# A planner's picture of its transfers: shared queues in place of fixed times

## The chip, the cores and the metric

The kernel runs on one core of a Trainium2 chip. The metric is the device time of one execution in microseconds (us), lower is better; a time is given as the median over runs.

## The reference

Attention in which a query only sees keys of the same hash bucket, followed by a feed-forward block with a gate (float32; 4 batches, 8 heads, sequence 768, head size 64; 3072 tokens, model width 512, inner width 2048):

```python
q_bits, k_bits = (q @ proj > 0), (k @ proj > 0)          # 6 bits each
mask = bucket(q_bits)[..., :, None] == bucket(k_bits)[..., None, :]
scores = where(mask, q @ k.T / sqrt(64), -1e9)
x = (softmax(scores) @ v)                                # to (3072, 512)
h = x @ w_in                                             # (3072, 2048)
g = h * erf(softplus(h))
out = g @ w_out                                          # (3072, 512)
```

## The kernel before, in words

**Two stages.** The attention (`attention`, 16 pairs of heads) is followed by the feed-forward (`feed_forward`), which works through six tiles `t` of 512 tokens. Both are written as lists of operations, each with an engine, a cost, the operations that it needs and a function that emits its instructions. A planner plays the list, and the operations are emitted in the order in which they came up. As every engine works through its instructions in order, this emission order is the order of each engine; the real waits between engines come from the data. So a planner's costs and times are nowhere waited for: they only decide what stands ahead of what on PE, DVE, ACT, POOL and SP. The attention is ordered by `arrange`, the feed-forward by `by_need`.

**`by_need` (lines 198 to 304).** For a margin it works out backward from the order of TensorE's products when each operation is due (`dates`), then plays the list forward (`play`): whenever an engine is free, it takes of the operations that are open the one due first (TensorE: the one of the lowest rank). It does so for three margins with five rounds each and keeps the order whose last TensorE operation ends soonest in the play. An operation opens when the operations in its `after` have ended, plus `late` of each of these where it is on another engine or `far` is set. A transfer is an operation on SP or POOL (its cost is the time to issue it) whose `late` is the time until its data has landed.

**The first product** `x @ w_in` is done in Strassen's manner (Winograd's form): seven products P1 to P7 of half size, the chain P1, P6, P2, P7, P4, P5, P3. For tile 0 these are plain (line 1444). For tiles 1 to 5 each of the seven is split again into seven small products (`small`, line 1683: 8 TensorE matmul instructions each in the trace). Their weights are 7 blocks for each step of the chain, 35 steps in all. These blocks are formed once, kept in DRAM, and read back for each step:

- `presum_inner` (line 1545, DVE) forms four of the seven blocks in a staging buffer. There are three: two in free rooms of `h`, one in `wt`, and the seven steps use them as 0, 1, 2, 0, 1, 2, 2. So P2, P5 and P3 go through `wt`, and P5's sums must wait until P2's have left.
- `keep` (line 1548, POOL) sends these four blocks (1.05 MB) to `wi_dram`; `keep_outer` (lines 1552 and 1553, SP, two issues) the other three for P6, P7, P5 and P3. `behind` puts the `keep` of P2, P4, P5 and P3 behind the first `load_wi` in the list.
- `load_wi` (line 1652, SP) reads the seven blocks of a step (1.835 MB) into a ring of two places in `w_in_sb`. A place is free when the products of two steps earlier are done; for the first two, when the plain products are done.
- `presum_xi` (line 1665, POOL) forms the sums of `x` for a step. `add_small` (lines 1710 on ACT and 1713 on DVE) takes each small product out of PSUM into `h`; PSUM has few banks for them, so a product waits for the addition of an earlier one.
- `add_far` (line 1720, POOL) adds a block of P5's result into `h` by an accumulating transfer, twice in a tile, with 512 KB each.

**The gate** (`gate_ops`: `lead` at line 1832 and `factor` at line 1840 on ACT, `multiply` at line 1847 on DVE) works on quarters of `h`. **The second product** `g @ w_out` (`project`, line 1987; 4 matmul instructions for each operation) of tile t runs interleaved with the first product of tile t + 1; in the later tiles three of its seven products are split again (`project_small`, line 2143), whose weight sums are kept by `keep_b` (line 2077, POOL) and read by `load_b` (line 2081, SP). `combine` (lines 2028 and 2030) adds the results and sends them out on SP (line 2036). `load_x` (line 447, SP) reads the `x` of the next tile.

Before, each of these transfers has a fixed `late`: `load_wi` 8.5 us (12.0 the first), `keep` 5.0, `keep_outer` 4.5, `add_far` 7.0, `keep_b` 5.0, `load_b` 7.0, `load_x` 6.0, whatever else is in flight.

Of the kernel before, what the change touches and what calls it, by code (L numbers as in the profile page):

```python
# [93 lines left out]
class Op:  # L94
# [13 lines left out]
    far: bool = False  # L108
    near: tuple = ()
    port: bool = False  # L110


TABLE_LOAD = 1.28
# [3 lines left out]
ROUNDS = 5  # L117
SHARED = 0.54
LENIENCE = 0.3


def arrange(ops, rooms, patience=0.0):
# [75 lines left out]
def by_need(ops, rooms, begin=None):  # L198

    names = {op.name: op for op in ops}
    users, needs = {}, {}
    for op in ops:
        needs[op.name] = {a for a in op.after if a in names}
        for a in needs[op.name]:
            users.setdefault(a, []).append(op)

    def away(a, op):
        return 0.0 if a.engine == op.engine and not a.far else a.late  # L210

    def dates(products, margin):
        starts, t = {}, 0.0
        for op in products:
            starts[op.name] = t
            t += op.cost
        left = {name: len(n) for name, n in needs.items()}
        sorted_ops, free = [], [op for op in ops if not left[op.name]]
        while free:
            op = free.pop()  # L220
            sorted_ops.append(op)
            for user in users.get(op.name, ()):
                left[user.name] -= 1
                if not left[user.name]:
                    free.append(user)
        due = {}
        for op in reversed(sorted_ops):
            due[op.name] = min(
                [starts.get(op.name, float("inf"))]
                + [due[user.name] - away(op, user) - user.cost - margin for user in users.get(op.name, ())]  # L230
            )
        return due

    def play(due):
        missing = {name: len(n) for name, n in needs.items()}
        opened = {}
        at, released, running = {}, {}, {}
        rings = {ring: [] for ring in rooms}
        table, now, order, ended = "exp", 0.0, [], 0.0
        for op in ops:  # L240
            opened.setdefault(op.engine, [])
            if not missing[op.name]:
                opened[op.engine].append(op)
                at[op.name] = 0.0

        def start_of(op):
            ring = rings[op.take[0]] if op.take else ()
            room = rooms[op.take[0]] if op.take else 1
            return max(at[op.name], released.get(ring[-room], float("inf")) if len(ring) >= room else 0.0)

        def place(op):
            return (op.rank if op.engine == "PE" else (due[op.name], op.rank)), op.name

        while len(order) < len(ops) or running:
            after = float("inf")
            for engine, entries in opened.items():
                if engine in running or not entries:
                    continue
                starts = [(start_of(op), op) for op in entries]
                first = max(min(start for start, _ in starts), now, (begin or {}).get(engine, 0.0))  # L260
                if first == float("inf"):
                    continue
                if first > now + 1e-9:
                    after = min(after, first)
                    continue
                op = min((op for start, op in starts if start <= first), key=place)
                cost = op.cost
                if op.table and op.table != table:
                    table = op.table
                    cost += TABLE_LOAD  # L270
                entries.remove(op)
                running[engine] = [op, cost]
                order.append(op)
                if op.take:
                    rings[op.take[0]].append(op.take)
            both = all(engine in running and running[engine][0].port for engine in ("DVE", "POOL"))
            pace = {engine: SHARED if both and running[engine][0].port else 1.0 for engine in running}
            after = min([after] + [now + rest / pace[engine] for engine, (_, rest) in running.items()])
            assert after < float("inf")
            for engine in list(running):  # L280
                running[engine][1] -= (after - now) * pace[engine]
                if running[engine][1] > 1e-9:
                    continue
                op = running.pop(engine)[0]
                if engine == "PE":
                    ended = after
                for what in op.free:
                    released[what] = after + op.late
                for user in users.get(op.name, ()):
                    at[user.name] = max(at.get(user.name, 0.0), after + away(op, user))  # L290
                    missing[user.name] -= 1
                    if not missing[user.name]:
                        opened[user.engine].append(user)
            now = after
        return order, ended

    best = None
    for margin in MARGINS:
        order = sorted(ops, key=lambda op: op.rank)
        for _ in range(ROUNDS):  # L300
            order, ended = play(dates([op for op in order if op.engine == "PE"], margin))
            if best is None or ended < best[0] - 0.05:
                best = ended, order
    return best[1]
@with_exitstack
def kernel(
# [34 lines left out]
    small = ctx.enter_context(tc.tile_pool(name="small", bufs=3))  # L341
# [1010 lines left out]
    def feed_forward(pools, check, late):  # L1352
# [27 lines left out]
        def op(name, engine, cost, rank, fn, args, reads=(), writes=(), after=(), **more):  # L1380

            needs = set(after)
            for x in tuple(reads) + tuple(writes):
                if x in wrote:
                    needs.add(wrote[x])
            for x in writes:
                needs |= read.get(x, set())
            for x in reads:
                read.setdefault(x, set()).add(name)
            for x in writes:  # L1390
                wrote[x] = name
                read[x] = set()
            needs.discard(name)
            more.setdefault("late", dict(PE=0.4, DVE=0.3, ACT=0.3, POOL=0.35, SP=0.3)[engine])
            ops.append(
                Op(name, engine, cost, rank, lambda: fn(*args), after=tuple(sorted(needs, key=str)), **more)
            )
# [165 lines left out]
        def inner_ops():  # L1563
            for n, name in enumerate(CHAIN):
# [4 lines left out]
                for k in range(4):  # L1569
# [8 lines left out]
                        writes=rooms[k : k + 1],  # L1578
                        after=(("inner", name, k - 1),),
# [9 lines left out]
                    reads=rooms,  # L1589
                    writes=(("wi", name, 0),),  # L1590
                    after=behind(name, False),
                    late=5.0,
                    far=True,
                )
                if name in ("P6", "P7", "P5", "P3"):
                    op(
                        ("keep_outer", name),
                        "SP",
                        1.0,
                        (1, 0.4 + 0.05 * n),  # L1600
                        keep_outer,
                        (name,),
                        reads=both,
                        writes=(("wi", name, 1),),
                        after=behind(name, True),
                        late=4.5,
                        far=True,
                    )


# [111 lines left out]
        def load_ops(t, i):  # L1722
# [8 lines left out]
                reads=(("wi", CHAIN[i], 0), ("wi", CHAIN[i], 1)),  # L1731
                writes=(("ring", n % 2),)
                + (tuple(("w", name, n) for name in ("P1", "P2", "P4", "P7")) if n < 2 else ()),
                late=12.0 if (t, i) == (1, 0) else 8.5,
                far=True,
            )

        def chain_ops(t):
            for i, name in enumerate(CHAIN):
# [54 lines left out]
                if name == "P5":  # L1794
                    for fl in range(2):
# [7 lines left out]
                            (t, fl),  # L1803
                            reads=both,
                            writes=part(t, 3, fl),
                            late=7.0,
                            far=True,
                        )
                        op(
                            ("add_both", t, fl),  # L1810
# [358 lines left out]
        def second_ops(t):  # L2169
# [70 lines left out]
            def blocks_of(name):  # L2240
                if t == HALVES and not again:
                    for k in range(4):
# [19 lines left out]
                        reads=(("b",),),  # L2262
                        writes=(("mb", name),),
                        after=(("small", t + 2, 0, "Q1"),) if name == "M3" else (),
                        late=5.0,
                        far=True,
                    )
                    return

# [8 lines left out]
                    reads=(("mb", name),),  # L2278
                    writes=(("b",),),
                    after=(("small", t + 1, 0, "Q4"),) if apart else (),  # L2280
                    late=7.0,
                    far=True,
                )

            def sums(name, k):
# [48 lines left out]
            now = [0.0]  # L2334
# [48 lines left out]
        def x_ops(t):  # L2383
# [1 line left out]
            keys = tuple(("x", kh, th, t % 2) for kh in range(2) for th in range(2))  # L2385
            op(
                ("load", t), "SP", 1.2, (1, t - 0.95, 0), load_x, (t,),
                writes=keys, late=6.0, far=True, after=(("late", 2),) if t == 1 else (("small", t - 1, 1, "Q4"),),
            )
            for k, (what, reads, into) in enumerate(  # L2390
                (
# [188 lines left out]
```

## Time and profile before

| | |
|---|---|
| median of 3 runs | 876.32 us (875.31 to 877.17) |
| profiled execution | 875.59 us |
| its span | 873.8 us |
| granted TensorE clock over the span | 0.998 |
| DMA traffic | 157.67 MB, mean 180 GB/s |

Engines: PE is TensorE's matmul, PEld its weight load, DVE VectorE, ACT ScalarE, POOL GpSimd, SP SyncE; with a q behind it (SPq, POOLq) a name stands for the queue of instructions of that engine, where transfers are issued. A line such as `L1683` is the line of the kernel that emitted the instruction, `M<-i,w_in_sb` what it writes and reads. The attention takes the first 313 us of the span; the plain products of tile 0 (line 1444) run from 313 to 363, and the small products (line 1683) of tiles 1 to 5 with the second product of the tile before from there on. In a row of waits the numbers are the us in total, how often, and the longest. In a row of the timeline they are start and length in us; a group of instructions in a row overlaps the next by the pipelining of TensorE. In a row of the stretches each engine has its busy time and its count of instructions.

### The profile page before, as it was taken

What the parts mean: (1) busy time and instruction counts of PE and PEld (TensorE: products, weight loads), DVE (VectorE), ACT (ScalarE), POOL (GpSimd) and SP (SyncE); (2) the same over time, 40 slices, a digit from 0 to 9 for tenths busy, and PEclk for the clock granted to TensorE, in tenths of its full rate; (3) what the DMA queues carried; (4) which work ended last, traced back from release to release, by engine and by line L of the source; (5) the groups of instructions that cost most, each with busy time, mean ns of one, the idle gap of its engine ahead of it and who ended that gap; (6) DMA issues with size and microseconds to landing.
All of it is one profiled execution on the core that took longest, in us unless ns stands there. A gap on an engine that the chain in (4) does not pass through costs nothing.

```text
span 873.8 us, 15404 instructions
## 1 busy us (share of the span) xinstructions
PE 864.8 (99%) x6064; PEld 673.0 (77%) x6064; DVE 705.2 (81%) x898; ACT 638.8 (73%) x905; POOL 201.8 (23%) x274
## 2 busy tenths in 40 slices
PE   9999999999999999989999999999999999999997
PEld 5444544444454468889999999999999999999997
DVE  5999999999899799569768776599589858976871
ACT  6888888888888748876688456776795677667930
POOL 1111121111111000424245347223421323210000
PEclk9999999999999999999999999999999999999999
DMA  9566766555762245577565646855676557564311
GB/s 227 149 184 194 212 202 182 171 148 166 189 177 97 86 176 200 188 282 254 191 165 211 208 143 182 272 188 203 187 211 241 199 151 233 203 207 137 104 62 41
DMA packets 100690, 157.67 MB, mean 180 GB/s; under 512 B 35278, under 2 KB 48638, under 8 KB 99712
## 3 DMA queue, kind: packets, MB, share of 16 engines
q1 hardware_dynamic: 90976, 123.32, 45.3%
q0 software_dynamic: 9184, 32.81, 12.3%
q8 instruction: 50, 0.82, 0.4%
q10 hardware_dynamic: 448, 0.46, 0.2%
q14 instruction: 32, 0.26, 0.1%
HBM read 121.86 MB, written 29.46 MB: 173 GB/s over the span
## 4 chain that ended last, share of the span: by engine, by line
PE 93%; DMA 3%; DVE 2%; ACT 1%; issue 1%; POOL 0%; DVEq 0%
PE M L1683 23%; PE M L1987 19%; PE st L698 18%; PE av L783 14%; PE M L1444 6%; PE M L2143 6%; PE X L2143 3%; DMA w_in_sb<-wi_P 2%; PE bits L986 1%; DMA wi_P<-wt 1%; PE bits L827 1%; ACT w L1840 1%; PE warm L947 1%; DVE h L1906 0%; PE X L1987 0%
## 5 line engine op out<-in xcount | busy, mean ns | idle before, releaser
L1840 ACT ACTIVATE w<-w,cq 128x1024 f32<-128x1024 f32 x144 | 162.7, 1147 | 1.6
L1713 DVE TENSOR_TENSOR h<-M,h 128x512 f32<-128x512 f32 x161 | 109.3, 687 | 60.4 <-PE M L1683 57.5
L698 PE MATMUL st<-q,k 64*128 64x384 f32 x768 | 155.1, 483 | 0.0
L1683 PE MATMUL M<-area,w_in_sb 128*128 128x128 f32 x1120 | 147.6, 276 | 0.7 <-DMA w_in_sb<-wi_P 0.6
L1683 PEld LDWEIGHTS M<-area,w_in_sb 128*128 128x128 f32 x1120 | 142.1, 193 | 5.2 <-DMA w_in_sb<-wi_P 0.7
L1840 ACT ACTIVATE w<-h,cq 128x1024 f32<-128x1024 f32 x96 | 108.9, 1146 | 12.3 <-DVE h L1847 7.9
L1987 PE MATMUL M<-w_out_sb,h 128*128 128x256 f32 x464 | 114.4, 380 | 0.0
L1683 PE MATMUL M<-i,w_in_sb 128*128 128x128 f32 x840 | 111.8, 276 | 2.4 <-DVE h L1713 2.4
L1683 PEld LDWEIGHTS M<-i,w_in_sb 128*128 128x128 f32 x840 | 108.4, 193 | 6.5 <-DVE h L1713 2.8
L1987 PE MATMUL M<-wt,area 128*128 128x256 f32 x384 | 97.3, 380 | 0.0
L698 PEld LDWEIGHTS st<-q,k 64*128 64x128 f32 x768 | 68.5, 187 | 36.2 <-issue 34.9
L1987 PEld LDWEIGHTS M<-w_out_sb,h 128*128 128x128 f32 x464 | 81.7, 191 | 7.6
L771 DVE TENSOR_TENSOR area<-area 128x1536 f32<-128x1536 f32 (+1 forms) x46 | 79.2, 1721 | 6.9 <-ACT area L725 5.6
L1665 POOL TENSOR_TENSOR i<-area,i 128x128 f32<-128x128 f32 x70 | 46.8, 689 | 150.5 <-PE M L1683 149.6
L1847 DVE SCALAR_TENSOR_TENSOR e<-w,e 128x1024 f32<-128x1024 f32 x48 | 65.9, 1373 | 16.8 <-ACT w L1840 16.7
L725 ACT ACTIVATE e_even<-st 128x768 f32<-128x768 f32 x96 | 73.9, 821 | 0.4 <-PE st L698 0.3
L1847 DVE SCALAR_TENSOR_TENSOR h<-w,e 128x1024 f32<-128x1024 f32 x48 | 63.2, 1317 | 12.8 <-ACT w L1840 12.5
L725 ACT ACTIVATE area<-st 128x768 f32<-128x768 f32 x90 | 72.7, 811 | 0.3 <-PE st L698 0.3
L1832 ACT ACTIVATE e<-h 128x1024 f32<-128x1024 f32 x48 | 50.6, 1054 | 30.4 <-DVE h L1713 27.9
L1987 PEld LDWEIGHTS M<-wt,area 128*128 128x128 f32 x384 | 66.6, 191 | 5.6
L783 PE MATMUL av<-e_even,v 128*64 128x385 f32 x384 | 65.7, 490 | 0.0
L698 PE MATMUL st<-both 64*128 64x384 bf16 x384 | 63.1, 324 | 0.2 <-ACT e_even L725 0.2
(186 smaller groups left out, 1305.1 us busy)
## 6 DMA issues: line engine op xcount, KB each, us to landing
w_in_sb<-wi_P SPq DMA_DIRECT2D x35, 1792.0 KB
raw<-in_w_out_dram POOLq DMA_DIRECT2D x16, 512.0 KB, 4.4
raw<-in_w_in_dram POOLq DMA_DIRECT2D x14, 512.0 KB, 5.9
v<-in_v_dram SPq DMA_DIRECT2D x32, 192.0 KB
out_dram<-area SPq DMA_DIRECT2D x23, 256.0 KB
q<-in_qkT_dram SPq DMA_DIRECT2D x30, 192.0 KB
k<-in_qkT_dram SPq DMA_DIRECT2D x30, 192.0 KB
r<-rd SPq DMA_DIRECT2D x30, 192.0 KB
```

Source lines behind the costliest of these rows:

```text
L698: nc.tensor.matmul(out=st[:, ab, 0:HS], lhsT=d["k" + src][rows, keys], rhs=d["q" + src][rows, cols], start=(part == 0), stop=(part == 1),)
L725: nc.scalar.activation(out=e[:, :, 0:HS], in_=st[:, :, 0:HS], func=AF.Exp, scale=scale)
L771: nc.vector.tensor_tensor(out=into, in0=one, in1=two, op=ALU.add)
L783: nc.tensor.matmul(out=d["av", half][rows, 0:w], lhsT=d["v"][:, g * GC + c, rows], rhs=e[:, ab, 0:w], start=(g == 0 and c == 0), stop=(g = ...
L1444: nc.tensor.matmul(out=kept[where][:, u, :], lhsT=a[:, kc, f : f + P], rhs=b[:, kc, :], start=(first and u == 0 and kc == 0), stop=(end an ...
L1683: nc.tensor.matmul(out=out_[:, c, :], lhsT=ring[:, W_AT[q], n % 2, c * P : (c + 1) * P], rhs=x, start=((q in ("Q1", "Q5") or q == "Q2" and ...
L1713: nc.vector.tensor_tensor(out=out_, in0=bank_, in1=one, op=ALU.add)
L1832: nc.scalar.activation(out=s, in_=unit(t, q, fl), func=AF.Silu)
L1840: nc.scalar.activation(out=st["q", t, q, fl, j], in_=f, func=func, scale=scale, bias=cq[:, column : column + 1])
L1847: nc.vector.scalar_tensor_tensor(out=unit(t, q, fl) if last else s, in0=st.pop(("q", t, q, fl, j)), scalar=GATE_S[j][1], in1=s, op0=ALU.ad ...
L1987: nc.tensor.matmul(out=where[:, sub, :], lhsT=a[:, j // G, j % G, sub * P : (sub + 1) * P], rhs=b[:, j, :], start=first, stop=end, skip_gr ...
L2143: nc.tensor.matmul(out=where[:, n * P : n * P + P], lhsT=a[:, j, :], rhs=b[:, j, :], start=(q in ("Q1", "Q2") and j == 0), stop=(q in ("Q4 ...
```

## The change

`Op` gets a field `mb`, the MB of a transfer. In `play`, a transfer with `mb` goes into a queue of its engine (SP's or POOL's) when its issue has ended. Only the head of each queue moves; the queues that are not empty share 0.322 MB/us evenly. When the head has moved all its MB, it leaves the queue, and its users open 1.9 us later (`LANDING`). For the due dates a transfer's `late` is 1.9 us and its MB at the full 0.322. All seven kinds of transfer of the feed-forward's list above get an `mb` and lose their fixed `late`; the four steps that end the attention (`late`, 0 to 2 among them with transfers), and the results that `combine` sends out, are not in the queues. The instructions of the kernel stay the same; their order is what the new play gives.

The last lines of the diff are, in this order, those of `keep`, `keep_outer`, `load_wi`, `add_far`, `keep_b`, `load_b` and `load_x`.

```diff
+    mb: float = 0.0
...
+LANDING = 1.9
+MB_PER_US = 0.322
...
+        queues = {}
+
+        def open_users(op, when):
+            for user in users.get(op.name, ()):
+                at[user.name] = max(at.get(user.name, 0.0), when(user))
+                missing[user.name] -= 1
+                if not missing[user.name]:
+                    opened[user.engine].append(user)
...
             after = float("inf")
+            flow = MB_PER_US / max(1, sum(1 for queue in queues.values() if queue))
...
-            after = min([after] + [now + rest / pace[engine] for engine, (_, rest) in running.items()])
+            after = min(
+                [after]
+                + [now + rest / pace[engine] for engine, (_, rest) in running.items()]
+                + [now + queue[0][1] / flow for queue in queues.values() if queue]
+            )
...
-                for user in users.get(op.name, ()):
-                    at[user.name] = max(at.get(user.name, 0.0), after + away(op, user))
-                    missing[user.name] -= 1
-                    if not missing[user.name]:
-                        opened[user.engine].append(user)
+                if op.mb:
+                    queues.setdefault(op.engine, []).append([op, op.mb, after])
+                    continue
+                open_users(op, lambda user: after + away(op, user))
+            for queue in queues.values():
+                if not queue or queue[0][2] > now:
+                    continue
+                queue[0][1] -= (after - now) * flow
+                if queue[0][1] < 1e-9:
+                    op = queue.pop(0)[0]
+                    open_users(op, lambda user: after + LANDING)
...
+            if more.get("mb"):
+                more.update(late=LANDING + more["mb"] / MB_PER_US, far=True)
...
-                    late=5.0,
+                    mb=1.05,
-                        late=4.5,
+                        mb=0.79,
-                late=12.0 if (t, i) == (1, 0) else 8.5,
+                mb=1.835,
-                            late=7.0,
+                            mb=1.05,
-                        late=5.0,
+                        mb=0.79,
-                    late=7.0,
+                    mb=0.79,
-                writes=keys, late=6.0, far=True, after=(("late", 2),) if t == 1 else (("small", t - 1, 1, "Q4"),),
+                writes=keys, mb=1.05, after=(("late", 2),) if t == 1 else (("small", t - 1, 1, "Q4"),),
```

More of the change, by code (lines that the diff above doesn't have):

```diff
@@ L1591, in inner_ops @@
                     after=behind(name, False),
-                    late=5.0,
-                    far=True,
+                    mb=1.05,
                 )
@@ L1605, in inner_ops @@
                         after=behind(name, True),
-                        late=4.5,
-                        far=True,
+                        mb=0.79,
                     )
@@ L1733, in load_ops @@
                 + (tuple(("w", name, n) for name in ("P1", "P2", "P4", "P7")) if n < 2 else ()),
-                late=12.0 if (t, i) == (1, 0) else 8.5,
-                far=True,
+                mb=1.835,
             )
@@ L1805, in chain_ops @@
                             writes=part(t, 3, fl),
-                            late=7.0,
-                            far=True,
+                            mb=1.05,
                         )
@@ L2264, in blocks_of @@
                         after=(("small", t + 2, 0, "Q1"),) if name == "M3" else (),
-                        late=5.0,
-                        far=True,
+                        mb=0.79,
                     )
@@ L2280, in blocks_of @@
                     after=(("small", t + 1, 0, "Q4"),) if apart else (),
-                    late=7.0,
-                    far=True,
+                    mb=0.79,
                 )
```

## The prediction, made before the changed kernel was run

> **What bounds the kernel now.** The page comes first, its busy times and its chain of work that ended last.
>
> ```profile
> PE 864.8 (99%) x6064; PEld 673.0 (77%) x6064; DVE 705.2 (81%) x898; ACT 638.8 (73%) x905; POOL 201.8 (23%) x274
> ...
> PE 93%; DMA 3%; DVE 2%; ACT 1%; issue 1%; POOL 0%; DVEq 0%
> ```
>
> TensorE is busy for 864.8 of the 873.8 us span. The change adds no instruction and takes none away, it only reorders them, so the 864.8 us stay but for what the clock does to them. What a new order can win lies in the 9 us that are left. The waits of PE say what ends them:
>
> ```profile
> PE M L1683 <- DVE h L1713: 2.4, 1, 2.4
> PE warm L947 <- DVE ones L362: 1.0, 1, 1.0
> PE M L1683 <- DMA w_in_sb<-wi_P: 0.6, 1, 0.6
> PE st L698 <- ACT e_even L725: 0.2, 1, 0.2
> PE X L2143 <- DVE area L2161: 0.2, 1, 0.2
> ```
>
> The second and fourth are in the attention stage, which another planner orders (`arrange`, untouched). In the stage that the changed planner orders PE waits three times, 3.2 us in all, and 2.4 us of that is one wait for an addition on DVE. The rest of the 9 us is the start and the drain after the last product. So the question is that one wait. The chain between 360 and 384 us, in order of time (start, length, what):
>
> ```profile
> 366.57 9.87 DMA wi_P<-wt
> ...
> 377.80 0.69 DVE h L1713
> 378.50 0.04 issue
> 378.54 4.52 PE M L1683 x24
> ```
>
> Read upwards: PE restarts at 378.54 because an addition out of PSUM (L1713) ended at 378.49. That addition stood on DVE behind two `presum_inner` (L1545), and the first of these waited until 376.44 (366.57 + 9.87) for the buffer `wt`, which a transfer issued at 366.57 was still emptying. DVE is in order: its list said that the buffer would be free sooner. The timeline of DVE, then of PE, shows it (in brackets the idle time before):
>
> ```profile
> 371.56 1.22 DVE L1847 SCALAR_TENSOR_TENSOR e<-w,e 128x1024 f32<-128x1024 f32 x1
> 376.47 0.69 DVE L1545 TENSOR_TENSOR wt<-area 128x512 f32<-128x512 f32 x1 [3.70 <-DMA wi_P<-wt]
> 377.19 0.69 DVE L1545 TENSOR_TENSOR wt<-wt,area 128x512 f32<-128x512 f32 x1
> 377.80 1.28 DVE L1713 TENSOR_TENSOR h<-M,h 128x512 f32<-128x512 f32 x2
> ```
>
> ```profile
> 372.42 1.95 PE L1683 MATMUL M<-area,w_in_sb 128*128 128x128 f32 x16
> ...
> 378.54 2.07 PE L1683 MATMUL M<-i,w_in_sb 128*128 128x128 f32 x8 [2.45 <-DVE h L1713]
> 380.41 1.76 PE L1683 MATMUL M<-area,w_in_sb 128*128 128x128 f32 x8
> 382.01 1.06 PE L1683 MATMUL M<-i,w_in_sb 128*128 128x128 f32 x8
> 382.90 1.03 PE L1987 MATMUL M<-wt,h 128*128 128x256 f32 x4
> ```
>
> The products that the two additions read ended by 374.4 (372.42 + 1.95). DVE stood idle from 372.8 to 376.4, so both additions could have been done by about 375.8, before PE ran out at 376.1 (378.54 - 2.45).
>
> **The cost of that wait is more than its length.** After it the two products of 8 matmuls start at 378.54 and 380.41, and the next at 382.01: 3.47 us for two, where the following one of the same kind takes 0.89 (382.01 to 382.90). The granted clock in the stretches around (columns: stretch, length, busy time of PE, PEld, DVE, ACT, POOL, clock, DMA share, GB/s):
>
> ```profile
> 378.50:382.00 3.50, 3.46 (x16) 3.46 (x17) 3.50 (x5) 1.15 (x1) 1.24 (x2) 0.52 0.23 83
> 382.00:385.50 3.50, 3.50 (x30) 3.40 (x29) 2.09 (x3) 3.29 (x5) 2.57 (x4) 1.00 0.89 290
> ```
>
> The clock was 0.52 for 3.5 us behind the wait and 1.00 after, so 3.47 - 2 x 0.89 = 1.69 us went there (by the clock, 0.48 x 3.5 = 1.68). The wait costs 2.45 + 1.69 = 4.14 us. The Trainium skill (TensorE: Matmul & The Clock Gate, Part 1) lets the gate fall only after an idle window of about 3.4 us; by that rule a wait of 2.45 would have left the clock alone and would be worth 2.45. The trace disagrees: 0.52 after 2.45 us.
>
> **The change part by part.** *Why the list was wrong here.* The old list gave the transfer of `keep` of P2 0.87 us to issue and then a fixed 5.0. Issued at 366.57 it would have landed at 372.4, just when DVE fell idle in the trace (372.8), so the list filled that hole with `presum_inner`. It took 9.87, because of what else was in flight. The rows of SP and POOL, then the memory traffic of the 10 us in question with that of the 12 us ahead:
>
> ```profile
> 352.06 11.03 SPq L1652 DMA_DIRECT2D w_in_sb<-wi_P  x2
> 363.14 0.64 SPq L1552 DMA_DIRECT2D wi_P<-area  x1
> ```
>
> ```profile
> 363.77 0.46 POOL L1665 TENSOR_TENSOR area<-area 128x128 f32<-128x128 f32 x1 [6.65 <-DVE area L464]
> ...
> 366.57 0.58 POOL L1548 DMA_DIRECT2D wi_P<-wt  x1
> 367.15 0.53 POOL L1548 DMA_DIRECT2D wi_P<-h  x1
> ```
>
> ```profile
> 354.00:366.00 12.00, 12.00 (x60) 10.63 (x59) 8.40 (x15) 8.04 (x10) 5.04 (x7) 1.00 0.57 188
> 366.50:376.50 10.00, 9.60 (x64) 8.62 (x62) 1.86 (x3) 9.13 (x11) 3.84 (x9) 1.00 1.02 373
> ```
>
> *What the new picture makes of it.* By its two constants of the diff (0.322 MB/us over all queues, 1.9 us to land): the second load of `wi` (1.835 MB) goes out on SP at about 362.6 (the end of its row, less 0.5 for the issue) and has moved 1.55 MB by 367.4, when the `keep` joins on POOL's queue. Then each gets 0.161 MB/us; the load ends 1.8 us later, but the two `keep_outer` behind it, from 363.14 on (0.79 MB each), keep SP's queue full, so the 1.05 MB of the `keep` take 6.5 us: 373.9, landed at 375.8. The trace has 376.44. The old price missed by 4.0 us, the new one by 0.6. With 375.8 the two additions are ready first, and the list puts them first: the wait goes, gain 4.14.
>
> *What moves with it.* The first load of `wi`, issued at 352.06, drops from 12.0 to 0.1 + 5.7 + 1.9 = 7.7 (nothing shares its line then). `keep` of P2 and P4 stand behind it in the list (`behind`), so they open at about 359.8 instead of 364.2. POOL is idle for 6.65 us up to 363.77, so both may go out there, ahead of the third `presum_xi`, into a stretch with 0.57 of DMA share instead of one with 1.02. `wt` would then be free by about 366, and DVE has room for it, as it is busy for only 1.86 us of the 10 from 366.5. This makes the gain safer, not larger: PE can win no more there than its wait. PE's first `small` (365.39 in the trace, after three M1 products) may go ahead of these; that swaps equal work.
>
> *What stays priced much as before.* The other figures move by less than their error: a `keep_outer` 4.5 to 4.35, `load_x` 6.0 to 5.2, `load_b` 7.0 to 4.35, `add_far` 7.0 to 5.2 when alone and more when shared. For `add_far` (L1720) the trace has issue to landing, and who waited for it:
>
> ```profile
>   ACT e L1832: 2.1, 1
> DMA to landing us min/median/max: 4.9/6.5/10.2
> ```
>
> The new price with its issue is 6.0 alone and 9.3 shared, inside 4.9 to 10.2; the old 7.9 was one value for all. The order it gives can cost PE nothing or up to the 2.1 us that ACT waited here once. I take nothing, as PE's own waits show none by way of ACT in this stage. The 0.6 us wait for a load may go or stay, and the 0.2 too; I keep both. Cover: over the 490 us behind 384 PE waits 0.8 us in all under the cruder prices, so the list has slack there. If a new order uses it up, the price is that of a wait seen: 0.6 (short) to 4.14 (long enough for the clock).
>
> *The sum.* The profiled execution took 875.59 (span 873.8 and 1.8 around it): 875.59 - 4.14 = 871.45. The median of the runs, 876.32, lies 0.73 above it: 872.2.
>
> **The rivals.** *Only part is won.* A new wait of 1 to 2 us in the new order takes back some. Also here: the clock does not answer as it did, and only 2.45 go, 873.9, as the rule cited above has it. The clock row speaks against the latter. Together 873 to 874.5: chance 0.12.
>
> *The wait moves.* The transfers between 352 and 380 are the same 7.3 MB; sent earlier, `keep` of P2 and P4 share the line with the second load of `wi` instead. Sharing from 362.6 on, its 1.835 MB at 0.161 end at 374.0 and land at 375.9. In the trace PE needs it at 380.41 (the eighth `small`), without the wait at 377. One microsecond is not much cover: a PE wait of 2 to 4 with the clock's loss gives 874.6 to 878. The list now counts this sharing, which speaks against it. The case that the list comes out with `presum_inner` at the same place is also in here, 876.3. Chance 0.20.
>
> *Slower.* The picture is still too kind to loads beside the accumulating `add_far`. The chain has such a load, with its true length:
>
> ```profile
> 536.65 13.85 DMA w_in_sb<-wi_P
> ```
>
> ```profile
> 537.91 0.88 POOL L1720 DMA_DIRECT2D h<-area  x1
> ```
>
> The new picture has it alone until 538.8 (0.66 MB), then halved: 7.3 us more and 1.9, landed at 548.0, where the trace has 550.5. A list that trusts 548.0 puts products too early, 2.5 us in each of five tiles, 12.5 us. Net of the 4.14 that is 8.4: 884.7. It ends slower if more than (4.14 + 1.75) / 5 = 1.2 of each 2.5 us reaches PE. Against it: the old price (8.6) had this load land at 545.3, 5.2 too early, and PE lost 0.6. Chance 0.18, with other new waits of that size.
>
> **How the numbers follow.** The forecast, the wait gone and less than 1 us new, has 0.50; with the part gain 0.62 lies on the faster side, 0.20 within, 0.18 slower. The bound is 0.2%, 1.75 us, about what a measurement of this kernel can tell from no change. The likeliest is 872.2. The low end takes the other 0.8 us along and a spread like that of the runs before (875.31 to 877.17, 1 us to a side): 870.6. The high end leaves out the slower case alone: 878.1. The first case alone spans 870.6 to 873.2.
>
> **What would show it.** In the profile after: no PE wait on L1713 near 376, no stretch with a clock near 0.5 behind 370, DVE's 3.7 us wait on `wi_P<-wt` gone, `keep` of P2 (L1548 on `wt`) issued by about 360. Step wrong if the `keep` stays at 366 and the additions still stand behind L1545. Forecast wrong if PE's waits behind 360 us sum to more than 2 us, above all on `w_in_sb<-wi_P`.

## The result, and the profile after

The changed kernel takes 870.97 us (median of 4 runs, 869.72 to 871.11) against 876.33 (875.31 to 877.17) for the kernel before: 5.36 us less, ratio 0.9938 with a 95% interval of 0.9922 to 0.9953. In a later group of runs it was 870.18 against 874.61: 4.43 us less, ratio 0.9952 (0.9940 to 0.9964). The kernel before took 874.4 to 875.3 in three later groups, so the second difference is nearer to the size of the gain than the first. Lines have moved by 21 to 25: L1706 is the small product (L1683 before), L1736 its addition (L1713), L1570 `presum_inner`, L1573 `keep`, L1675 `load_wi`, L1648 `presum_w`.

The page after, busy times and chain; its span is 869.2 us:

```profile
PE 861.8 (99%) x6064; PEld 671.4 (77%) x6064; DVE 702.5 (81%) x898; ACT 638.2 (73%) x905; POOL 197.7 (23%) x274
...
PE 97%; DMA 1%; POOL 0%; issue 0%; ACT 0%; DVE 0%; POOLq 0%
```

The chain had 3% of DMA and 2% of DVE before, and has 1% and nothing now. The waits of PE (us in total, times, longest):

```profile
PE M L1706 <- DVE h L1736: 1.5, 1, 1.5
PE warm L970 <- DVE ones L385: 1.0, 1, 1.0
PE st L721 <- ACT e_even L748: 0.2, 1, 0.2
```

The 2.4 us wait, the 0.6 for a load and the 0.2 have gone; one of 1.5 us is new. The place of the old wait, on DVE and then on PE:

```profile
374.33 0.69 DVE L1736 TENSOR_TENSOR h<-M,h 128x512 f32<-128x512 f32 x1 [1.94 <-PE M L1706]
374.94 1.21 DVE L1868 SCALAR_TENSOR_TENSOR e<-w,e 128x1024 f32<-128x1024 f32 x1
376.07 0.68 DVE L1736 TENSOR_TENSOR h<-M,h 128x512 f32<-128x512 f32 x1
...
383.71 0.68 DVE L1570 TENSOR_TENSOR wt<-area 128x512 f32<-128x512 f32 x1
```

```profile
373.17 1.95 PE L1706 MATMUL M<-area,w_in_sb 128*128 128x128 f32 x16
374.95 1.03 PE L2008 MATMUL M<-wt,h 128*128 128x256 f32 x4
375.82 1.05 PE L1706 MATMUL M<-i,w_in_sb 128*128 128x128 f32 x8
376.71 1.06 PE L1706 MATMUL M<-area,w_in_sb 128*128 128x128 f32 x8
```

The additions stand first, DVE waits for PE and no longer for a transfer, and the first `presum_inner` of P5 follows at 383.71, without a wait for `wt`. PE runs through, and so does its clock (stretches as before; the clock is the number behind the engines):

```profile
374.00:378.00 4.00, 4.00 (x35) 3.90 (x34) 3.55 (x4) 3.79 (x5) 0.98 (x1) 1.00 1.02 421
378.00:382.00 4.00, 4.00 (x30) 3.79 (x30) 1.32 (x3) 3.97 (x5) 1.49 (x4) 1.00 0.30 110
```

What is new stands 40 us later. The chain there:

```profile
404.28 10.74 DMA wi_P<-wt
415.02 0.02 issue
415.04 0.04 DVE wt L1648
415.08 1.15 issue
416.22 0.69 DVE h L1736
416.91 0.14 issue
417.05 1.02 PE M L1706 x7
```

It is the old mistake once more with other names: a `presum_w` waits for the `keep` of P3 to leave `wt`, and an addition stands behind it. PE idles for 1.49 us, and the clock stays at 1.00 this time.

The gain by place, from the starts of PE's instructions (the time from one start to the next, less what the same pair of forms takes elsewhere): the kernel before lost 4.28 us near 378, 0.38 near 414, 0.78 near 550 and 0.59 near 826; the changed one loses 1.71 near 417 and nothing at the others. 6.03 - 1.71 = 4.3, of 4.6 us between the two spans.

### The profile page after: what moved, and what is told of

It reads as the page before. It is cut to its first block, busy times and chain, and to the rows that moved or that the text cites. A ratio compares the mean times of both kernels' runs of the same rounds, so it can differ in the third digit from the quotient of the medians.

```text
span 869.2 us, 15388 instructions
## 1 busy us (share of the span) xinstructions
PE 861.8 (99%) x6064; PEld 671.4 (77%) x6064; DVE 702.5 (81%) x898; ACT 638.2 (73%) x905; POOL 197.7 (23%) x274
## 3 DMA queue, kind: packets, MB, share of 16 engines
q0 software_dynamic: 9184, 32.81, 12.2%
## 4 chain that ended last, share of the span: by engine, by line
PE 97%; DMA 1%; POOL 0%; issue 0%; ACT 0%; DVE 0%; POOLq 0%
PE M L1706 24%; PE M L2008 21%; PE st L721 18%; PE av L806 15%; PE M L2164 6%; PE M L1469 6%; PE X L2164 4%; PE bits L1009 1%; DMA wi_P<-wt 1%; PE bits L850 1%; PE warm L970 1%; PE X L2008 0%; PE bits L540 0%; POOL i L1688 0%; PE z_ps L850 0%
## 5 line engine op out<-in xcount | busy, mean ns | idle before, releaser
L1736 DVE TENSOR_TENSOR h<-M,h 128x512 f32<-128x512 f32 x161 | 109.7, 687 | 57.4 <-PE M L1706 56.5
L1706 PE MATMUL M<-area,w_in_sb 128*128 128x128 f32 x1120 | 146.4, 275 | 0.0
L1706 PEld LDWEIGHTS M<-area,w_in_sb 128*128 128x128 f32 x1120 | 141.3, 192 | 3.8
L1706 PE MATMUL M<-i,w_in_sb 128*128 128x128 f32 x840 | 110.3, 275 | 1.5 <-DVE h L1736 1.5
L1706 PEld LDWEIGHTS M<-i,w_in_sb 128*128 128x128 f32 x840 | 106.8, 192 | 5.1 <-issue 1.9
```

What stands on the lines that cost most here:

```text
L1706: nc.tensor.matmul(out=out_[:, c, :], lhsT=ring[:, W_AT[q], n % 2, c * P : (c + 1) * P], rhs=x, start=((q in ("Q1", "Q5") or q == "Q2" and ...
L1736: nc.vector.tensor_tensor(out=out_, in0=bank_, in1=one, op=ALU.add)
```

## The experiments

Theory A: the gain is the order on DVE where it waits for `wt`, so that an addition that PE needs no longer stands behind a wait for a transfer. Rival B: the gain comes from transfers sent at other times, with less on the line. Rival C: a search among many orders made a lucky draw, and the faithful picture has nothing to do with it. Each experiment was timed with several runs beside the kernel before, which took 875.30 us in the first group (e1 to e4), 874.40 in the second (e5 to e8) and 874.61 in the third.

**e1, the additions first.** The list of before with one move, everything else as it was:

```diff
         listed = by_need(ops, dict(e=2, w=2), dict(DVE=3.4) if late else None)
+        if not again:
+            names = [each.name for each in listed]
+            moved = [each for each in listed if each.name in (("inner", "P5", 0), ("inner", "P5", 1))]
+            listed = [each for each in listed if each not in moved]
+            at = [each.name for each in listed].index(("add_small", 1, 0, "Q3")) + 1
+            listed[at:at] = moved
```

> The kernel before, with one edit of its list: the first two presum_inner of P5 go behind the two additions Q7 and Q3 of the first step that they stood ahead of. Prices, and the order of all else, are those of before. Theory A (the order at this one place is the gain): the 2.45 us wait of PE near 376 and the 0.52 clock behind it both go, 4.1 us: 872.2, and the small waits near 413, 550 and 827 stay. Rival B (the gain comes from transfers sent at other times): no change, 876.3.

872.14 against 875.30, ratio 0.9972 (0.9961 to 0.9983): 3.2 us less, with no transfer moved in the list. B is out as the main cause. The forecast wait has gone, but not all of its price. PE, ACT and DVE:

```profile
378.27 1.03 PE L1987 MATMUL M<-wt,h 128*128 128x256 f32 x4
380.93 1.16 PE L1683 MATMUL M<-i,w_in_sb 128*128 128x128 f32 x8 [1.62 <-ACT M L1460]
```

```profile
379.24 1.15 ACT L1840 ACTIVATE w<-h,cq 128x1024 f32<-128x1024 f32 x1 [3.60 <-DVE h L1847]
380.30 0.58 ACT L1460 COPY M<-M 128x512 f32<-128x512 f32 x1
```

```profile
376.08 0.69 DVE L1545 TENSOR_TENSOR wt<-area 128x512 f32<-128x512 f32 x1 [1.32 <-DMA wi_P<-wt]
...
377.73 1.48 DVE L1847 SCALAR_TENSOR_TENSOR h<-w,e 128x1024 f32<-128x1024 f32 x1
```

DVE still waits for `wt`, now behind the additions; a multiplication of the gate stands behind that, ACT waits for it, and the copy that PE needs stands behind on ACT. Two in-order engines carry the wait on to PE, 1.62 us of it, and the clock does not fall. The wait for a load near 550 also grew, from 0.55 to 1.07 us. So A holds for the wait at 376, and is too narrow: the sums have to go behind the gate's work too, as they do in the changed kernel.

**e2, the sum back in front.** The changed kernel, with the first of the two sums put back ahead of the additions, by the same code:

```diff
+            moved = [each for each in listed if each.name in (("inner", "P5", 0),)]
...
+            at = [each.name for each in listed].index(("add_small", 1, 0, "Q7")) + 0
```

> The changed kernel, with the first presum_inner of P5 put back ahead of the addition Q7 of the first step. Theory A: DVE waits for the transfer out of wt again. It is issued at 369.9 here and traffic ends near 379, so PE, which runs out of work at about 376, stands until about 381: 5 us of wait and 1.7 of clock, 877 to 878. Rival B: the transfers are as in the changed kernel, so the time stays at 871.

878.48 against 875.30, ratio 1.0041 (1.0027 to 1.0055). PE waits 5.9 us, longer than in the kernel before, because the `keep` of P2 is issued at 369.9 in place of 366.6. The clock falls at 378.2, inside the wait, and is back at 385.1 (rows: the waits of PE, then two stretches):

```profile
PE M L1706 <- DVE h L1736: 5.9, 1, 5.9
```

```profile
376.00:381.80 5.80, 0.00 (x0) 0.00 (x0) 1.27 (x3) 0.57 (x1) 0.00 (x0) 0.69 0.54 221
381.80:385.30 3.50, 3.42 (x17) 3.42 (x18) 2.89 (x4) 1.15 (x1) 1.20 (x2) 0.54 0.00 0
```

One instruction moved by eight places in DVE's order costs more than the whole change gains. A is confirmed; the time is a little above the 877 to 878 expected, with a wait of 5.9 us where 5 were expected.

**e3, the wait filled.** The kernel before, with work for PE while it waits; the extra products go to a bank that nobody reads:

```diff
+        def fill():
+            for _ in range(10):
+                nc.tensor.matmul(
+                    out=kept["X"][0:D, 0:P],
+                    lhsT=ones,
+                    rhs=ones[:, 0:1].broadcast_to([P, P]),
+                    start=True,
+                    stop=True,
+                )
+
+        if not again:
+            at = [each.name for each in listed].index(("small", 1, 0, "Q4"))
+            listed.insert(at, Op(("fill",), "PE", 2.3, (0, 0), fill))
```

> The kernel before, with twenty matmul instructions on ones (about 2.3 us at full clock) put on PE into the wait near 376; they write a bank that nobody reads, the results are not changed. The wait for DVE stays. Theory A on its second term (the clock falls because PE idles for 2.45 us): the clock stays at 1.00 and 1.7 us are saved, 874.6. Rival (the clock falls for another reason, or 2.45 us of idle time are too short to matter): the 0.5 stretch of 3.4 us stays, 876.3 or a little more.

874.03 against 875.30, ratio 0.9986 (0.9976 to 0.9996): 1.3 us less, although PE gets 20 more instructions and its next products start at 378.1, hardly sooner than the 378.5 of the kernel before. The stretch behind them:

```profile
378.30:381.80 3.50, 3.50 (x29) 3.40 (x30) 3.50 (x5) 2.21 (x4) 1.51 (x3) 1.00 0.43 105
```

The clock is 1.00 there, against 0.52 before. The mean clock of all 11 timed executions is 0.999 or 1.000; of the 17 of the kernel before in this group, 9 have 0.998 or less. So the fall of the clock is caused by the idle PE, and the second term of the prediction's sum is real.

**e4, the new wait.** The changed kernel with the `presum_w` that waits near 413 behind the additions:

```diff
+            moved = [each for each in listed if each.name in (("presum_w", 0, 3),)]
...
+            at = [each.name for each in listed].index(("add_small", 1, 3, "Q4")) + 1
```

> The changed kernel, with one presum_w (the one that waits 2.47 us for the transfer of P3 out of wt near 413) moved behind the two additions that stand behind it. Theory A (the same mistake once more, with the new picture 1.7 us short): the last PE wait of 1.5 us goes and nothing else changes, 869.5. Rival (PE's wait moves to the next addition, or DVE is full there): 870.5 to 871.

870.51 against 875.30, ratio 0.9947 (0.9934 to 0.9961); not to be told from the changed kernel by the time. The trace says why: the 1.5 us went, and 1.0 came at nearly the same place, for the next load of `wi`:

```profile
415.03 1.13 PE L1706 MATMUL M<-area,w_in_sb 128*128 128x128 f32 x8 [0.97 <-DMA w_in_sb<-wi_P]
```

The rival was right that the wait moves, though not to an addition. The move need not have brought the wait for the load: in e9 the changed kernel itself waits for it at 414.45, for 1.3 us. The two waits lie together, and which of them ends last differs between executions.

**e5, queues for `keep` alone.** All other transfers get back their fixed times:

```diff
-                mb=1.835,
+                late=12.0 if (t, i) == (1, 0) else 8.5,
+                far=True,
...
```

> The changed kernel with queues for keep alone; all other transfers have the fixed times of before. The keep of P2 is then pictured with its line to itself, and the list puts one sum of P5 ahead of the addition Q7 and one between Q7 and Q3, with the transfer sent as late as before. Theory A (what matters is that SP's load is seen on the same line): PE still waits near 376, 1.7 to 2.5 us with or without the clock's 1.7, so 0 to 2 us below the kernel before. Rival (the price of keep alone was wrong): 4 us below it.

874.75 against 874.40, ratio 0.9995 (0.9983 to 1.0008): nothing gained. DVE waits for `wt` as before, and PE behind it:

```profile
DVE wt L1570 <- DMA wi_P<-wt: 3.7, 1, 3.7
```

```profile
PE M L1707 <- DVE h L1737: 2.6, 1, 2.6
```

By the new constants a `keep` on a line of its own takes 1.05 / 0.322 + 1.9 = 5.2 us, nearly the old 5.0, and the list is as wrong. So the price of the `keep` by itself was not what was missing; the load on SP's queue beside it was. e8 shows the same from the other side: a load that shares its line with a `keep` is late.

**e6, queues for all but `keep`.** The `keep` has its fixed 5.0 us again:

```diff
-                    mb=1.05,
+                    late=5.0,
+                    far=True,
```

> The changed kernel with the old fixed 5.0 us for keep and queues for the rest. The first load of wi is then pictured alone on its line, the keep of P2 and P4 come 7 us sooner in the list (as my prediction had it for the full change), and the sums of P5 too. Theory A (any order in which DVE does not wait for wt ahead of an addition gains): the transfer lands near 367, before DVE asks, 3 to 4 us below the kernel before. Rival (a fixed price for keep leaves the wait): as before, within 1 us.

869.34 against 874.40, ratio 0.9945 (0.9933 to 0.9957): 5.1 us less, the most of the second group. The transfers of P2 and P4 go out at 356.81 and 357.39, 12 to 13 us sooner than in the changed kernel, and PE has no wait left behind the attention:

```profile
356.81 0.58 POOL L1573 DMA_DIRECT2D wi_P<-wt  x1
357.39 0.53 POOL L1573 DMA_DIRECT2D wi_P<-h  x1
363.52 0.46 POOL L1689 TENSOR_TENSOR area<-area 128x128 f32<-128x128 f32 x1 [5.61 <-DVE area L487]
```

Here the wait goes by another way: the first sum of P5 still stands ahead of the additions, and the buffer is free in time.

**e7, a longer fixed time.** The kernel before with one number changed, no queues:

```diff
-                    late=5.0,
+                    late=9.0,
```

> The kernel before with one number changed: 9.0 us for keep in place of 5.0, no queues. The list then puts the sums of P5 behind the additions, at about the place that the changed kernel has them less 5 us. Theory A: 3.5 to 4.5 us below the kernel before, the queues are not needed for this gain. Rival (it takes the queues, since a longer time for every keep pushes others into new waits): less than 2 us.

871.11 against 874.40, ratio 0.9966 (0.9953 to 0.9978): 3.3 us less, a little under what was expected. The queues are not needed for the larger part of the gain: a fixed time near the measured 9.9 us does it.

**e8, the collision behind the new wait.** The changed kernel with the move of e4, and:

```diff
+            moved = [each for each in listed if each.name in (("keep", "P3"),)]
...
+            at = [each.name for each in listed].index(("presum", 2, 1)) + 1
```

> The changed kernel with two moves in its list: the keep of P3 goes behind the two presum_x that follow it on POOL (issued near 409 in place of 404.5), and the presum_w that waits for it behind two additions, as in the run before. If the PE wait of 1.0 us for a load that took the place of the 1.5 us wait there comes from sharing the line with this keep, both go, 1.5 us below the changed kernel: 869.5. Rival (the load would be late without it too): 870.5.

869.51 against 874.40, ratio 0.9946 (0.9933 to 0.9958). Both waits near 415 have gone, with the `keep` issued at 408.96 in place of 404.28. So the load was late because it shared the line with this `keep`. One PE wait is left, 1.0 us for a load at 725.9; e4's profile has it too (at 727.1), the changed kernel's two profiles do not. I have not found what brings it. The time is 4.9 us below before, within the scatter of the changed kernel's 4.4 to 5.4.

**e9 to e12, the changed kernel beside three others.** e9 is the changed kernel, e10 is e6 once more, and e11 and e12 change one constant (to 0.29 in e12):

```diff
-MB_PER_US = 0.322
+MB_PER_US = 0.4
```

> The changed kernel once more, beside the next three on one chip. Its only PE wait behind 360 us in the profile was 1.5 us near 417. Expected 4.0 to 5.4 us below the kernel before.

> The kernel with queues for all transfers but keep (fixed 5.0) once more. Its profile had no PE wait at all behind the attention, against 1.5 us in the changed kernel. If waits are all that separates the orders, it is 1.5 us below the changed kernel in this call; if not, within 0.5 us of it.

> The changed kernel with 0.40 MB/us in place of 0.322, a picture a quarter too fast. Its list has one sum of P5 between the additions Q7 and Q3, with the keep of P2 sent 5.8 us sooner than in the changed kernel. Theory A (any order that lets the transfer land before DVE asks for wt): no wait near 376, 3 to 5 us below the kernel before. Rival (only a picture at the measured speed gives such an order, else a new wait of 2 us or more comes up): 0 to 2.5 us below.

> The changed kernel with 0.29 MB/us in place of 0.322, a picture a tenth slower. The list has the sums of P5 behind the additions, as with 0.322. Theory A: 3.5 to 5.5 us below the kernel before. Rival (the gain of the changed kernel is one lucky draw of a search that scatters): 0 to 2.5 us below.

| | median, us | range | ratio to before (95%) | waits of PE behind 360 us |
|---|---|---|---|---|
| before | 874.61 | 873.24 to 876.29 | | 3.2 (first profile) |
| e9, 0.322 | 870.18 | 870.11 to 870.87 | 0.9952 (0.9940 to 0.9964) | 1.3 |
| e10, all but `keep` | 869.28 | 868.86 to 870.19 | 0.9941 (0.9929 to 0.9953) | none |
| e11, 0.40 | 869.93 | 869.60 to 870.35 | 0.9948 (0.9936 to 0.9960) | 0.4 |
| e12, 0.29 | 869.41 | 868.70 to 870.32 | 0.9941 (0.9929 to 0.9953) | none |

The constants a quarter up and a tenth down do as well as the chosen one. In that range, C's lucky draw is not needed and an exact picture is not either. e10 and e12 lie 0.8 to 0.9 us below the changed kernel in the same group, by about the PE wait that it has (1.3) and they have not; I expected 1.5. They are the best versions found; the intervals overlap, so the step from the changed kernel to them is small and not certain.

## Why the prediction was right, and where it was not

The time, 870.97, lies in the range (870.6 to 878.1), 1.2 us below the forecast of 872.2. From one profiled execution to the other the gain is 4.5 us (875.59 to 871.11), against the 4.14 forecast. The rest of the 5.36 comes from the median of the kernel before, which was 0.73 above its profiled execution and higher than in any later group.

*The wait and its cause* held. The wait near 376 has gone, because the additions went ahead of `presum_inner` (profile after), and putting one back costs about 8 us (e2 at 1.0041 of the time before, the changed kernel at 0.9938 and 0.9952). That the price of the `keep` was wrong for lack of the load beside it holds too, as far as e5 and e8 show it.

*The price of the wait* held for the execution that was profiled: 2.45 and 1.69, and e3 shows the second to be caused by the idle time. For a median it is too large a term. Each timed execution comes with its mean granted clock. Of 45 of the kernel before in the three groups, 23 have 0.999 or 1.000 and take 874.0 us in the mean, 22 have 0.998 or less and take 875.3. In e5, which has a wait of 2.6 us at the same place, 4 with 0.999 or more lie at 871.3 to 872.4 and 8 with less at 873.8 to 875.4. So the clock seems to fall in some executions and not in others, and the profiled one was of the dearer kind. The split is rough: the mean also counts the drain behind the last product (e10, which has no such wait, has one execution at 0.998), and the 3 us between the two kinds of e5 are more than the clock's term, which leaves a part unexplained.

The traces show what decides it. In every profile the granted clock changes only at whole steps of 3.413 us: in the kernel before it was full for 372.053 us (109 steps), half for 3.413 (1) and full for 491.519 (144); in e2 the half clock lasted 6.827 (2). What counts is how long PE was busy within one step:

| profile | step | PE busy, of 3.41 us | clock behind the step |
|---|---|---|---|
| e5 | 373.56 to 376.97 | 0.94 | falls |
| before | 375.06 to 378.47 | 1.03 | falls |
| e2 | 374.82 to 378.23 | 1.15 | falls |
| e7, drain at the end | 863.40 to 866.81 | 1.33 | falls |
| e3, drain at the end | 865.87 to 869.29 | 1.41 | stays |
| e1 | 377.83 to 381.24 | 1.79 | stays |
| after | 415.67 to 419.08 | 2.03 | stays |

So in these traces the clock falls when PE is idle for more than about 2.05 us of one step. A wait of 2.45 us has that much in one step for 3.41 - 2.45 + 2 x (2.45 - 2.05) = 1.76 of the 3.41 us over which its start can lie. That is about half, as an estimate; 22 of the 45 executions had the lower clock. The sum took the 1.69 as certain.

The rule that I cited against the trace (the Trainium skill, TensorE: Matmul & The Clock Gate, Part 1) says in the same place that its window runs freely and that cold stretches vary from run to run; that part agrees. Its idle window of about 3.4 us does not agree as a condition: PE was idle for 2.4 us of one step (3.41 - 1.03) when the clock fell here.

*What moves with it* failed. I had the first load of `wi` alone on its line, and so the `keep` of P2 and P4 sent by about 360. They went out at 369.30 and 369.88, later than before, and P4 ahead of P2:

```profile
369.30 0.58 POOL L1573 DMA_DIRECT2D wi_P<-h  x1
369.88 0.53 POOL L1573 DMA_DIRECT2D wi_P<-wt  x1
```

In the list the `keep` of P7 stands just ahead of that load and shares its line, though in the trace it has been sent 18 us before (334.94 against 353.07): `behind` holds it back in the play alone. I read the trace for what is in flight, where the play counts. With `keep` out of the queues (e6) the step comes out as I wrote it, 356.81. I had called it a safety and no gain. e10 lies 0.9 us below e9, but e12, where that `keep` goes out at 368.5 and the sums stand behind the additions, lies 0.8 below too; so a gain from the earlier `keep` is not shown.

*The other terms.* I took nothing for the rest. It was 0.38 + 0.78 + 0.59 = 1.75 us saved near 414, 550 and 826, and 1.71 lost to the new wait near 417, so nothing net, by two errors of the same size: that is luck. The new wait belongs to the first rival, a new wait of 1 to 2 us: the mechanism came, and only its cover by the other gains kept the sum.

*The rivals.* The wait that moves to a load (0.20) did not come in the changed kernel's first profile but is close: 1.3 us at 414.45 in e9, 1.0 in e4. The slower case (0.18), loads beside `add_far` priced too short, did not show: the wait near 550 that it was built on has gone.

## What to carry to other kernels

On engines that work in order, a planner's price for a transfer decides what stands behind a wait; it matters only where an operation that the busiest engine needs is put behind it, so look for that one place in the waits before reworking the model. Price a transfer with what shares its line, on all queues together, or leave it the time measured in company (e7). After a reordering, look for the next place where the same mistake stands: it came back at once, 40 us later.

## What the runs showed of the hardware

The granted clock of PE changed only at whole steps of 3.413 us. It fell behind steps in which PE was busy for 1.33 us or less, and stayed full behind those with 1.41 or more. So one wait of 2.45 us (before) or 2.61 (e5) cost one step at half clock, one of 5.91 (e2) two, of which the first lay inside the wait, and waits of 1.49 (after) and 1.62 (e1) none. Filling the idle time with useless products kept the clock up and paid for itself (e3, 1.3 us less). A `keep` of about 1 MB landed in 4.1 to 4.9 us at four places of the kernel before and in 9.0 to 12.2 at the other three; two of these were issued as a stretch with a DMA share of 1.02 began (366.5 to 376.5).
